# A hand-ordered attention kernel: the transposes of the score maxima, the last maximum and some conversions of operands and weights stand at other places of the order

## The chip, the cores and the metric

The kernel runs on one core of one Trainium2 chip. The metric is device time in microseconds of one execution; lower is better. "Before" ran three times: 929.05, 930.24 and 933.62 us, median 930.24 us.

## The reference: what is computed

Bucketed attention over 4 batches of 8 heads (768 positions, head size 64), then a feed-forward layer whose activation is a quotient of two polynomials.

```python
q_bits = (einsum('bhsd,dk->bhsk', q, proj) > 0)          # 6 bits, likewise k_bits
q_bucket = sum(q_bits * 2 ** arange(6), axis=-1)          # likewise k_bucket
mask = q_bucket[:, :, :, None] == k_bucket[:, :, None, :]
scores = where(mask, scale * q @ k.T, -1e9)
attn = exp(scores - max(scores)); attn = attn / (sum(attn) + 1e-9)
x = (attn @ v) as rows of B*S tokens by H*D
h = x @ w_in;  P = a0 + a1 h + a2 h^2 + a3 h^3;  Q = 1 + |b0||h| + |b1|h^2
out = (P / (Q + 1e-6)) @ w_out
```

`w_in` and `w_out` arrive as 64-bit floats and are taken apart on the chip into a high and a low fp32r part; so are q and k.

## The kernel before

**Work units.** The 32 heads are 16 pairs `p` (two heads each). A pair has 12 score steps `s` (two halves of the queries, six blocks of 128 keys) and 12 maximum steps (two heads, six blocks of 128 queries). Four kinds of TensorE work alternate:

- `scores(p, s)`: for each head two matmuls (high parts with the rows of mask and shift, then the cross terms) into one PSUM buffer `pss`; ScalarE then takes the exponential into `E`; GpSimd adds the exponentials into `acc`.
- `maxstep(p, j)`: two matmuls of high parts into a PSUM buffer `psm`, which VectorE reduces to column `j` of `m`. The maxima of pair p+1 are taken while the scores of pair p run.
- `values(p, s)`: `psv` accumulates V times `E`; the steps 0 to 5 are one group of matmuls, 6 to 11 the other.
- `shift_turn(p)`: TensorE transposes `m` (128x12) into `pst`; VectorE clamps and negates it into `mt`; `shift_rows(p)` is a DMA that puts `mt` into row 76 of q, where the scores of pair p find it.

**PSUM buffers decide what may start.** `psm` (and `psb` of the bits) come from the pool `ps_a`, which has two buffers: the matmul of one maximum can be issued when the reduction of the maximum two before it has ended. `pss`, `pst` and `psu` share the tag "s" of the pool `ps_b`, which has three buffers: a `pss` can be issued when the exponential (or, for a `pst`, the clamping) three allocations before it has ended.

**The order is written out.** All steps are put into a dictionary `plan` under a position `12 * p + s` (function `at`, lines 476 to 477; `spread` for generators), with `s` from the tables `MID`, `FIRST`, `LAST`; at the end (lines 589 to 591) the positions are run in rising order. Each engine executes its own instructions in that order, and so does SyncE, which issues nearly all DMAs. An entry such as `shift_turn=8.61` therefore means: in program order between the scores 8 and 9 of the pair before.

**Names that the change touches.** `maxima` and `maxima_steps` (positions of the twelve maxima relative to the pair two before); `low` (its second number: the subtraction that makes the low part of k, `lo<-qkf,k` on VectorE); `shift_turn` and `shift_rows`; and `weights`, two lists of positions for the generator `weights(i)` at lines 432 to 470. Even `i` is a piece of `w_in`: DMA, two ScalarE conversions with a VectorE mask (`wr<-wr`), a VectorE shift-and-or (`ws<-ws,wr`), an integer add (`CUSTOM_DVE`, `ISA` in the order), the ScalarE cast into `wi_hi`, the VectorE subtraction into `wi_lo`. Odd `i` is a piece of `w_out`; its subtraction is `wr<-ws,wr`, after which `wo_d<-wr` stores both parts. There is one piece of each in every pair.

Of the kernel before, what the change touches and what calls it, by code (L numbers as in the profile page):

```python
# [39 lines left out]

MID = dict(
    group=6, values=[0.66, 0.05], values_out=3.5, maxima=7.17,
    maxima_steps=[0, 1.15, 1.73, 2.64, 3.32, 5.08, 5.86, 6.98, 8.0, 8.84, 10.26, 11.37], sums=14.65, sums_store=17.37,
    high=[-0.41, 1.19], low=[1.06, 3.35], bits=2.81, penalties=4.05, high_move=1.9, maskrows=5.61, second_low=-2.2,
    second_high=2.69, load_v=10.99, shift_turn=8.61, shift_rows=8.82, load=9.0, recips=[20.0, 22.0, 23.0],
    weights=[[1.44, 4.0, 4.1, 5.09, 5.49, 7.11, 9.5, 9.75, 17.5], [8.05, 10, 10.65, 11.5, 12.38, 14.29, 16.34, 19.32, 21.22]],
    weights_last=[0.5, 0.8, 1.0, 1.2],
)

# [2 lines left out]
    high_move=4.53, maskrows=8.2, second_low=4.25, second_high=4.35, load_v=4.78, group=2,  # L52
    values=[2.35, 2.65, 2.32, 2.35, 0.35, 0.61], values_out=3.02, high1=[-0.27, -5.58], low1=[11.24, 4.95],
    high_move1=20.05, load2=21.89, load3=3.8, penalties1=-6.57, maskrows1=3.69,
    weights=[[-5.7, 6.64, 6.7, 11.42, 12.19, 18.75, 21.75, 38.77, 44.13], [8.03, 9.04, 9.24, 11.12, 14.81, 15.27, 15.99, 17.91, 46.81]],
    warm=6, warms=[3, 3, 3, 1, 1, 1], maxima00=[-4.26, -2.29, -4.17, 1.67, -1.15, 2.77], shift00=[2.15, 4.99],
    shift0=[3.67, 3.44], ahead=3, scores=[[3.68, 3.82, 7.26], [6.03, 8.25, 12.4]], pen01=[4.77, 14.55], comp01=3.35,
    second_high0=[-2.86, 2.12, -3.42, 3.45], load_v0=20.9, bits1=5.23, comp1=[15.82, 11.68],
    maxima0=[3.11, -1.97, -0.5, 2.14, 2.86, 3.25], turn1=[8.46, 13.26], rows1=[9.59, 14.35],
)  # L60

LAST = dict(
# [2 lines left out]
    sums=16.96, wide=8, share=11, third=0, sums14=14.69, weights14=1.44, sumst14=22.46,  # L65
# [38 lines left out]
def bucket_attention_then_rational_ffn(ctx, tc, qT, kT, v, proj, w_in, w_out, coef, consts, out):  # L104
# [56 lines left out]
    def operands_to_terms():  # L161
# [3 lines left out]

    tail.tile([P, 32], F32, tag="below", name="below")
    last = attention(tc, nc, raw, ps_b, tail, tokens, early, operands_to_terms, ffn, load, QF, KF, v, w_in, w_out, wo_d, ident, cst,
                     ones, prj, wi_hi, wi_lo, x_d, s_d, r_d, coefficients)
    ffn.rest(ctx, last)
# [3 lines left out]
def attention(ctx, tc, nc, raw, ps_b, tail, tokens, early, operands_to_terms, ffn, load, QF, KF, v, w_in, w_out, wo_d, ident, cst, ones, prj,  # L173
# [243 lines left out]
    def recips(bb):  # L417
        n = 2 * NHP * S // P
        s = tail.tile([P, n], F32, tag="rs", name=f"rs{bb}")
        nc.sync.dma_start(s, s_d[bb].rearrange("h (x c) -> (h x) c", c=n))  # L420
        yield
        z = tail.tile([P, n], F32, tag="rz", name=f"rz{bb}")
        nc.vector.tensor_scalar(out=z, in0=s, scalar1=0.0, scalar2=S * TINY, op0=ALU.is_equal, op1=ALU.mult)
        nc.vector.tensor_tensor(out=z, in0=s, in1=z, op=ALU.add)
        nc.vector.tensor_scalar(out=s, in0=s, scalar1=0.0, scalar2=1e-9, op0=ALU.is_gt, op1=ALU.mult)
        nc.vector.tensor_tensor(out=z, in0=z, in1=s, op=ALU.add)
        nc.vector.reciprocal(out=s, in_=z)
        yield
        nc.sync.dma_start(r_d[bb].rearrange("h (x c) -> (h x) c", c=n), s)
        yield  # L430
# [45 lines left out]
    def at(p, s, f, *args):  # L476
        plan.setdefault(12 * p + s, []).append((f, args))

    def spread(p, steps, gen):
        for s in steps:  # L480
            at(p, s, lambda g: next(g, None), gen)

    for p in range(NPAIR):
        mid = 0 < p < NPAIR - 1
        n = MID["group"] if mid else (FIRST if p == 0 else LAST)["group"]
        for s in range(12):
            if p > 0 or s >= FIRST["ahead"]:
                at(p, s, scores, p, s)

            if p > 1:  # L490
                at(p - 2, MID["maxima"] + MID["maxima_steps"][s] if p > 2 else FIRST["maxima2"] + FIRST["rate2"] * s, maxstep, p, s)
            if s % n == n - 1:
                for i in range(s - n + 1, s + 1):
                    at(p, s + (MID["values"][s // n] if mid else (FIRST if p == 0 else LAST)["values"][s // n]), values, p, i)
            if s % NT == NT - 1:
                at(p, s + (LAST["vout14"] if (p, s) == (NPAIR - 2, 11) else MID["values_out"] if mid else (FIRST if p == 0 else LAST)["values_out"]), values_out, p, s // NT)
        for hf in range(2):
            at(p, 6 * hf + 9, values_store, p, hf)
        if p < NPAIR - 1:
            at(p, MID["sums"] if p < NPAIR - 2 else LAST["sums14"], sums, p)  # L500
            at(p, MID["sums_store"] if p < NPAIR - 2 else LAST["sumst14"], sums_store, p)
        if p > 1:
            for t in range(2):
                at(p - 2, (MID if p > 2 else FIRST)["high"][t], high, p, t)
                at(p - 2, (MID if p > 2 else FIRST)["low"][t], low, p, t, nc.vector if p > 2 else nc.gpsimd)
            if p % 2 == 0:
                at(p - 2, (MID if p > 2 else FIRST)["bits"], bits, p)
                at(p - 2, (MID if p > 2 else FIRST)["penalties"], penalties, p)
            at(p - 2, (MID if p > 2 else FIRST)["high_move"], high_move, p)
            at(p - 2, (MID if p > 2 else FIRST)["maskrows"], maskrows, p)  # L510
        if p > 0:
            at(p - 1, (MID if p > 1 else FIRST)["second_low"], second_low, p)
            at(p - 1, (MID if p > 1 else FIRST)["second_high"], second_high, p)
            at(p - 1, (MID if p > 1 else FIRST)["load_v"], load_v, p)
        if p > 1:
            at(p - 1, MID["shift_turn"], shift_turn, p)
            at(p - 1, MID["shift_rows"], shift_rows, p)
        if p > 3:
            at(p - 4, MID["load"], load, p)
        if p % NHP == NHP - 1 and p + 1 < NPAIR:  # L520
            spread(p, MID["recips"], recips(p // NHP))
# [308 lines left out]
```

## Time and profile before

| | us |
|---|---|
| median of three runs | 930.24 |
| lowest, highest | 929.05, 933.62 |
| the profiled execution | 929.79 |
| span of the profiled execution | 928.0 |

| stage of the span (us) | TensorE busy | VectorE busy | ScalarE busy | GpSimd busy |
|---|---|---|---|---|
| 0 to 40, start | 37.29 | 27.18 | 24.72 | 23.75 |
| 240 to 280, middle of the attention | 40.00 | 35.65 | 27.32 | 30.78 |
| 360 to 400, its last two pairs | 39.39 | 34.63 | 30.89 | 27.77 |
| 440 to 480, feed-forward layer | 40.00 | 39.40 | 28.99 | 9.68 |

A pair takes 24.4 us where the bits of two pairs are made in it and 23.1 us where they are not (in the middle of the attention the first maximum of a next pair starts at 206.85, 231.70 and 254.78 us). In the timeline a row is: start, length, engine, line, operation, output tile, input tile, shapes, how many instructions were joined; in brackets the idle time of that engine ahead of it and what ended it. Matmuls overlap, so the time that one costs is the distance from its start to the next start. The granted TensorE clock was full (1.00) all through.

### The profile page before, as it was taken

Reading aid. Unit: us, or ns where it says so; the run is one execution under the profiler, and the core shown is the slowest. Engines: PE = TensorE matmul, PEld = TensorE weight load, DVE = VectorE, ACT = ScalarE, POOL = GpSimd, SP = SyncE. Lnnn points to the kernel's source line nnn. Section 1 sums busy time; section 2 is a strip of 40 time slices with the busy share of each in tenths; the row PEclk is TensorE's granted clock in tenths of the full one; section 3 lists DMA queues with packets and bytes.
Section 4 is the critical chain, followed back from the end, with each engine's and each line's share of the span. In section 5 each row is a group of like instructions: output and inputs, shape, how many; then the busy total and the mean of one; then the engine's idle time right before and its main releaser. Section 6 shows DMA issues by size and latency. Waiting matters only on the chain.

```text
span 928.0 us, 13694 instructions
## 1 busy us (share of the span) xinstructions
PE 920.8 (99%) x4678; PEld 699.9 (75%) x4678; DVE 842.0 (91%) x1029; ACT 647.6 (70%) x1229; POOL 435.8 (47%) x361
## 2 busy tenths in 40 slices
PE   8999999999999999999999999999999999999998
PEld 4666766666767676668888888888888888888886
DVE  6799889888988898888998999899999999998996
ACT  6567767676767766887767766776676677667664
POOL 5587878787788877622222232223222322232221
PEclk9999999999999999999999999999999999999999
DMA  6767878878877777545402100400040003001001
GB/s 197 214 181 219 229 230 230 223 214 212 242 212 225 229 195 233 163 155 197 163 1 81 56 1 1 136 2 0 1 137 1 1 34 102 1 1 46 1 1 46
DMA packets 51098, 111.57 MB, mean 120 GB/s; under 512 B 9330, under 2 KB 19942, under 8 KB 51028
## 3 DMA queue, kind: packets, MB, share of 16 engines
q1 hardware_dynamic: 50596, 110.34, 40.5%
q8 instruction: 37, 0.61, 0.3%
q10 hardware_dynamic: 432, 0.36, 0.1%
q14 instruction: 33, 0.27, 0.1%
HBM read 56.82 MB, written 21.17 MB: 84 GB/s over the span
## 4 chain that ended last, share of the span: by engine, by line
PE 93%; DVE 4%; DMA 1%; SPq 0%; ACT 0%; issue 0%; DVEq 0%; ACTq 0%
PE psh L93 28%; PE pso L93 28%; PE pss L93 14%; PE psv L93 12%; PE psm L93 7%; PE psu L93 2%; DVE m L93 2%; DMA wr<-w_in 1%; PE psb L93 1%; DVE ws L93 1%; DVE wr L93 0%; SPq L93 0%; PE psw L93 0%; PE pst L93 0%; ACT E L93 0%
## 5 line engine op out<-in xcount | busy, mean ns | idle before, releaser
L93 POOL TENSOR_TENSOR gl<-c,gh 128x512 fp32r<-128x512 f32 x95 | 133.2, 1402 | 387.0 <-ACT gh L93 371.0
L93 ACT ACTIVATE E<-pss 128x384 f32<-128x384 f32 x384 | 167.5, 493 | 105.8 <-PE pss L93 91.9
L93 PE MATMUL pso<-wo,gh 128*128 128x512 f32 x768 | 236.2, 390 | 0.0
L93 DVE TENSOR_REDUCE m<-psm 128x1 f32<-128x768 f32 x192 | 179.5, 948 | 31.4 <-PE psm L93 28.2
L93 POOL TENSOR_TENSOR acc<-E,E 128x384 f32<-128x384 f32 x124 | 155.6, 1273 | 85.9 <-ACT E L93 85.7
L93 PE MATMUL pss<-q,k 128*128 128x384 f32 (+2 forms) x768 | 171.3, 347 | 0.3 <-ACT E L93 0.3
L93 PEld LDWEIGHTS pso<-wo,gh 128*128 128x128 f32 x768 | 144.3, 188 | 29.9
L93 PEld LDWEIGHTS pss<-q,k 128*128 128x128 f32 (+2 forms) x768 | 134.6, 190 | 29.1 <-issue 17.0
L93 PE MATMUL psh<-xh,wi_hi 128*128 128x512 f32 x384 | 149.8, 390 | 0.0
L93 PE MATMUL psh<-xl,wi_hi 128*128 128x512 f32 x384 | 149.7, 390 | 0.0
L93 PE MATMUL psh<-xh,wi_lo 128*128 128x512 f32 x384 | 149.6, 390 | 0.0
L93 PE MATMUL pso<-wo,gl 128*128 128x512 f32 x384 | 149.1, 390 | 0.0
L93 ACT ACTIVATE h<-psh 128x512 f32<-128x512 f32 x96 | 57.4, 598 | 130.5 <-PE psh L93 130.3
L93 POOL TENSOR_TENSOR acc<-acc,E 128x384 f32<-128x384 f32 x123 | 136.6, 1129 | 5.9 <-ACT E L93 5.7
L93 DVE SCALAR_TENSOR_TENSOR c<-c,ab,r 128x512 f32<-128x512 f32 x96 | 135.6, 1413 | 0.0
L93 PE MATMUL psv<-E,v 128*64 128x385 f32 x768 | 131.9, 492 | 0.0
L93 PE MATMUL psm<-k,q 76*128 76x384 f32 (+1 forms) x384 | 102.4, 349 | 1.6 <-DVE m L93 1.0
L93 PEld LDWEIGHTS psv<-E,v 128*64 128x64 f32 x768 | 52.2, 137 | 65.3 <-issue 63.7
L93 DVE SCALAR_TENSOR_TENSOR w<-h,absb,w 128x512 f32<-128x512 f32 x96 | 74.0, 771 | 16.2 <-ACT w L93 15.9
L93 PEld LDWEIGHTS psh<-xh,wi_hi 128*128 128x128 f32 x384 | 72.1, 188 | 16.1 <-issue 1.2
L93 PEld LDWEIGHTS psh<-xh,wi_lo 128*128 128x128 f32 x384 | 72.2, 188 | 14.9
L93 PEld LDWEIGHTS psh<-xl,wi_hi 128*128 128x128 f32 x384 | 72.1, 188 | 14.9
(78 smaller groups left out, 1221.3 us busy)
## 6 DMA issues: line engine op xcount, KB each, us to landing
q<-q SPq DMA_DIRECT2D x45, 192.0 KB
k<-k SPq DMA_DIRECT2D x45, 192.0 KB
wr<-w_in SPq DMA_DIRECT2D x16, 512.0 KB
wr<-w_out SPq DMA_DIRECT2D x16, 512.0 KB
wo_d<-wr SPq DMA_DIRECT2D x16, 512.0 KB
wo<-wo_d SPq DMA_DIRECT2D x16, 512.0 KB
qkf<-qT SPq DMA_DIRECT2D x16, 384.0 KB
qkf<-kT SPq DMA_DIRECT2D x16, 384.0 KB
```

The costliest lines, as they stand in the source:

```text
L93: return self.tc.keep_in_program_order(issue(*args, **kwargs))
```

## The change

Only positions change; no instruction is added or removed.

```diff
 MID = dict(
-    maxima_steps=[0, 1.15, 1.73, 2.64, 3.32, 5.08, 5.86, 6.98, 8.0, 8.84, 10.26, 11.37], sums=14.65, sums_store=17.37,
-    high=[-0.41, 1.19], low=[1.06, 3.35], bits=2.81, ...
-    second_high=2.69, load_v=10.99, shift_turn=8.61, shift_rows=8.82, load=9.0, recips=[20.0, 22.0, 23.0],
-    weights=[[1.44, 4.0, 4.1, 5.09, 5.49, 7.11, 9.5, 9.75, 17.5], [8.05, 10, 10.65, 11.5, 12.38, 14.29, 16.34, 19.32, 21.22]],
+    maxima_steps=[0, 1.15, 1.73, 2.64, 3.32, 5.08, 5.86, 6.98, 8.0, 8.84, 10.26, 10.45], sums=14.65, sums_store=17.37,
+    high=[-0.41, 1.19], low=[1.06, 5.64], bits=2.81, ...
+    second_high=2.69, load_v=10.99, shift_turn=5.67, shift_rows=7.2, load=9.0, recips=[20.0, 22.0, 23.0],
+    weights=[[1.44, 5.63, 5.65, 5.7, 6.3, 8.3, 10.2], [8.05, 10, 10.65, 11.5, 12.38, 14.29, 17.645, 19.32, 21.22]],
 FIRST = dict(
-    ... rows1=[9.59, 14.35],
+    ... rows1=[9.59, 14.35], turn2=8.61, rows2=8.82,
...
-            at(p - 1, MID["shift_turn"], shift_turn, p)
-            at(p - 1, MID["shift_rows"], shift_rows, p)
+            at(p - 1, MID["shift_turn"] if p > 2 else FIRST["turn2"], shift_turn, p)
+            at(p - 1, MID["shift_rows"] if p > 2 else FIRST["rows2"], shift_rows, p)
```

The twelfth maximum moves from 7.17 + 11.37 - 12 = 6.54 to 7.17 + 10.45 - 12 = 5.62 of the pair before; the first group of values stands at 5 + 0.66 = 5.66, the transpose now at 5.67. Pairs 3 to 15 are transposed at the new place (13 transposes); pairs 0 to 2 stay.

On TensorE, around the first group of values in pair 3 (its scores are `pss_6_0` for step 6 and head 0, with `q_3` and `k_3`; `psm` are the maxima of pair 4, and of pair 5 from `psm_0` on; `psv_0` are the values; "x2" is two matmuls), there stood before, from the last matmuls of the group on:

```order
L93 MATMUL psv_0_1316<-E_153,v_1161 64x385 x2
L93 MATMUL pss_6_0_1329<-q_3_614,k_3_651 128x384
L93 MATMUL pss_6_0_1329<-q_3_852,k_3_853 128x384
L93 MATMUL pss_6_1_1333<-q_3_614,k_3_651 128x384
L93 MATMUL pss_6_1_1333<-q_3_852,k_3_853 128x384
L93 MATMUL psm_11_1337<-k_4_938,q_4_906 128x384 x2
L93 MATMUL pss_7_0_1341<-q_3_614,k_3_651 128x384
L93 MATMUL pss_7_0_1341<-q_3_852,k_3_853 128x384
L93 MATMUL pss_7_1_1345<-q_3_614,k_3_651 128x384
L93 MATMUL pss_7_1_1345<-q_3_852,k_3_853 128x384
L93 MATMUL psm_0_1354<-k_5_1219,q_5_1187 128x384 x2
```

and now, first ahead of the values and then from the last matmuls of the group on:

```order
L93 MATMUL psm_9_1284<-k_4_938,q_4_906 128x384 x2
L93 MATMUL pss_5_0_1288<-q_3_614,k_3_651 128x384
L93 MATMUL pss_5_0_1288<-q_3_851,k_3_852 128x384
L93 MATMUL pss_5_1_1292<-q_3_614,k_3_651 128x384
L93 MATMUL pss_5_1_1292<-q_3_851,k_3_852 128x384
L93 MATMUL psm_10_1300<-k_4_938,q_4_906 128x384 x2
L93 MATMUL psm_11_1308<-k_4_938,q_4_906 128x384 x2
L93 MATMUL psv_0_1318<-E_148,v_1161 64x385 x2
```

```order
L93 MATMUL psv_0_1318<-E_153,v_1161 64x385 x2
L93 MATMUL pst_None<-cst,m_1087 12x128
L93 MATMUL pss_6_0_1336<-q_3_614,k_3_651 128x384
L93 MATMUL pss_6_0_1336<-q_3_851,k_3_852 128x384
L93 MATMUL pss_6_1_1340<-q_3_614,k_3_651 128x384
L93 MATMUL pss_6_1_1340<-q_3_851,k_3_852 128x384
L93 MATMUL pss_7_0_1345<-q_3_614,k_3_651 128x384
L93 MATMUL pss_7_0_1345<-q_3_851,k_3_852 128x384
L93 MATMUL pss_7_1_1349<-q_3_614,k_3_651 128x384
L93 MATMUL pss_7_1_1349<-q_3_851,k_3_852 128x384
L93 MATMUL psm_0_1357<-k_5_1219,q_5_1187 128x384 x2
```

Where in pair 3 the second and third maximum of pair 5 stand there was before (and now the row `pst` is gone from there):

```order
L93 MATMUL pss_8_1_1363<-q_3_614,k_3_651 128x384
L93 MATMUL pss_8_1_1363<-q_3_852,k_3_853 128x384
L93 MATMUL psm_1_1372<-k_5_1219,q_5_1187 128x384 x2
L93 MATMUL pst_None<-cst,m_1084 12x128
L93 MATMUL psm_2_1385<-k_5_1219,q_5_1187 128x384 x2
```

`psm_11` moved from between the scores of steps 6 and 7 to directly behind `psm_10`, ahead of the values, so that the four scores 6_0, 6_1, 7_0 and 7_1 now follow each other without a maximum; the transpose `pst` stands behind the values. Its old neighbours `psm_1` and `psm_2` now follow each other directly.

On VectorE, from the ninth maximum of pair 4 on, there stood before (`lo_5` is the low part of k of pair 5, `wr_1100` and `wr_1221` pieces of `w_out` and `w_in`):

```order
L93 TENSOR_REDUCE m_1084<-psm_8_1269 128x1
L93 TENSOR_TENSOR lo_5_1273<-qkf_847,k_5_1219 128x768
L93 TENSOR_REDUCE m_1084<-psm_9_1287 128x1
L93 TENSOR_SCALAR wr_1221<-wr_1221 128x512
L93 TENSOR_TENSOR wr_1100<-ws_1101,wr_1100 128x512
L93 SCALAR_TENSOR_TENSOR ws_1222<-ws_1222,wr_1221 128x512
L93 TENSOR_REDUCE m_1084<-psm_10_1307 128x1
L93 ISA ws_1222<-wr_1221,ws_1222 128x1024
L93 TENSOR_REDUCE m_1084<-psm_11_1337 128x1
L93 TENSOR_REDUCE m_1353<-psm_0_1354 128x1
L93 TENSOR_REDUCE m_1353<-psm_1_1372 128x1
L93 TENSOR_SCALAR mt_None<-pst_None 12x128
```

and there stands now:

```order
L93 TENSOR_REDUCE m_1087<-psm_8_1269 128x1
L93 TENSOR_REDUCE m_1087<-psm_9_1284 128x1
L93 TENSOR_REDUCE m_1087<-psm_10_1300 128x1
L93 TENSOR_REDUCE m_1087<-psm_11_1308 128x1
L93 TENSOR_TENSOR lo_5_1313<-qkf_847,k_5_1219 128x768
L93 TENSOR_TENSOR wr_1104<-ws_1105,wr_1104 128x512
L93 TENSOR_SCALAR wr_1221<-wr_1221 128x512
L93 TENSOR_SCALAR mt_None<-pst_None 12x128
L93 SCALAR_TENSOR_TENSOR ws_1222<-ws_1222,wr_1221 128x512
L93 ISA ws_1222<-wr_1221,ws_1222 128x1024
L93 TENSOR_REDUCE m_1356<-psm_0_1357 128x1
```

The four reductions stand together ahead of the low part and the weights, and the clamping `mt` stands ahead of the shift-and-or.

On ScalarE, behind the exponentials of step 7 of pair 3, the cast `wi_hi` stood ahead of the exponentials of step 8; now it stands behind them, directly ahead of the two instructions that take out the values (`col`, `xo`):

```order
L93 ACTIVATE E_149<-pss_8_0_1363 128x384
L93 ACTIVATE E_149<-pss_8_1_1367 128x384
L93 CAST wi_hi<-ws_1222 128x512
L93 COPY col_0_1381<-psv_0_1318 128x1
L93 ACTIVATE xo_0_1382<-psv_0_1318,col_0_1381 128x384
L93 ACTIVATE E_150<-pss_9_0_1389 128x384
```

The first two ScalarE conversions of the `w_in` piece moved likewise, from ahead of the exponentials of step 5 to behind them. On SyncE the DMA of the row of maxima (`q<-mt`) now stands ahead of the store `wo_d<-wr` and of the next load of `w_out`; before, it stood behind both.

More of the change, by code (lines that the diff above doesn't have):

```diff
@@ L42 @@
     group=6, values=[0.66, 0.05], values_out=3.5, maxima=7.17,
-    maxima_steps=[0, 1.15, 1.73, 2.64, 3.32, 5.08, 5.86, 6.98, 8.0, 8.84, 10.26, 11.37], sums=14.65, sums_store=17.37,
-    high=[-0.41, 1.19], low=[1.06, 3.35], bits=2.81, penalties=4.05, high_move=1.9, maskrows=5.61, second_low=-2.2,
-    second_high=2.69, load_v=10.99, shift_turn=8.61, shift_rows=8.82, load=9.0, recips=[20.0, 22.0, 23.0],
-    weights=[[1.44, 4.0, 4.1, 5.09, 5.49, 7.11, 9.5, 9.75, 17.5], [8.05, 10, 10.65, 11.5, 12.38, 14.29, 16.34, 19.32, 21.22]],
+    maxima_steps=[0, 1.15, 1.73, 2.64, 3.32, 5.08, 5.86, 6.98, 8.0, 8.84, 10.26, 10.45], sums=14.65, sums_store=17.37,
+    high=[-0.41, 1.19], low=[1.06, 5.64], bits=2.81, penalties=4.05, high_move=1.9, maskrows=5.61, second_low=-2.2,
+    second_high=2.69, load_v=10.99, shift_turn=5.67, shift_rows=7.2, load=9.0, recips=[20.0, 22.0, 23.0],
+    weights=[[1.44, 5.63, 5.65, 5.7, 6.3, 8.3, 10.2], [8.05, 10, 10.65, 11.5, 12.38, 14.29, 17.645, 19.32, 21.22]],
     weights_last=[0.5, 0.8, 1.0, 1.2],
@@ L58 @@
     second_high0=[-2.86, 2.12, -3.42, 3.45], load_v0=20.9, bits1=5.23, comp1=[15.82, 11.68],
-    maxima0=[3.11, -1.97, -0.5, 2.14, 2.86, 3.25], turn1=[8.46, 13.26], rows1=[9.59, 14.35],
+    maxima0=[3.11, -1.97, -0.5, 2.14, 2.86, 3.25], turn1=[8.46, 13.26], rows1=[9.59, 14.35], turn2=8.61, rows2=8.82,
 )
```

## The prediction, made before the changed kernel ran

> **What bounds the kernel now.** I read the page's busy times first, then the timelines of TensorE, VectorE and ScalarE over two pairs in the middle of the attention.
>
> ```profile
> PE 920.8 (99%) x4678; PEld 699.9 (75%) x4678; DVE 842.0 (91%) x1029; ACT 647.6 (70%) x1229; POOL 435.8 (47%) x361
> ```
>
> TensorE works 99% of the span. A wait that the change puts in front of one of its instructions lengthens the kernel by its whole size, and a wait that it takes away shortens it; nothing else on the other engines counts unless TensorE waits for it. So the question is which TensorE instruction of the new order finds its buffer still taken. The TensorE rows of one pair, from its tenth maximum to the fourth one of the next pair (psm_9, psm_10, values, scores 6, psm_11, scores 7, psm_0, scores 8, psm_1, transpose, psm_2, scores 9, psm_3):
>
> ```profile
> 247.35 0.52 PE L93 MATMUL psm<-k,q 76*128 76x384 f32 x2
> ...
> 248.42 0.52 PE L93 MATMUL psm<-k,q 76*128 76x384 f32 x2
> 248.87 4.10 PE L93 MATMUL psv<-E,v 128*64 128x385 f32 x24
> 252.90 0.97 PE L93 MATMUL pss<-q,k 77*128 77x384 f32 x4
> 253.71 0.52 PE L93 MATMUL psm<-k,q 76*128 76x384 f32 x2
> 254.07 0.87 PE L93 MATMUL pss<-q,k 77*128 77x384 f32 x4
> 254.78 0.52 PE L93 MATMUL psm<-k,q 76*128 76x384 f32 x2
> 255.13 0.87 PE L93 MATMUL pss<-q,k 77*128 77x384 f32 x4
> 255.84 0.52 PE L93 MATMUL psm<-k,q 76*128 76x384 f32 x2
> 256.20 0.27 PE L93 MATMUL pst_None<-cst,m 128*12 128x128 f32 x1
> 256.34 0.62 PE L93 MATMUL psm<-k,q 76*128 76x384 f32 x2
> 256.80 0.87 PE L93 MATMUL pss<-q,k 77*128 77x384 f32 x4
> 257.51 0.51 PE L93 MATMUL psm<-k,q 76*128 76x384 f32 x2
> ```
>
> From start to start a maximum costs 0.36 us, four score matmuls 0.71, the group of values 4.03, the first scores behind it 0.81. One place is already at its limit, the psm_2 behind the transpose:
>
> ```profile
> 255.33 0.96 DVE L93 TENSOR_REDUCE m<-psm 128x1 f32<-128x768 f32 x1
> ...
> 256.34 0.19 PEld L93 LDWEIGHTS psm<-k,q 76*128 76x128 f32 x1 [0.23 <-DVE m L93]
> ```
>
> The reduction of psm_0 starts 0.55 after psm_0 (254.78 to 255.33), takes 0.96, and ends at 256.29; the weight load of psm_2, which takes over its buffer, starts at 256.34. So with VectorE idle and waiting, **a maximum may start 0.55 + 0.96 + 0.05 = 1.56 us after the one two before it**. A maximum that had to wait starts together with its weight load, and the next instruction follows 0.46 later (256.34 to 256.80) instead of 0.36.
>
> **Term 1, psm_11 directly behind psm_10.** From psm_9 to psm_10 are 1.07 us (247.35 to 248.42), so psm_11 would start at 1.43 and what follows it at 1.79. Its buffer is that of psm_9: it may start at 1.56, and what follows it at 2.02. That is 0.23 lost, if the reduction of psm_9 starts at once. VectorE's rows say that it will:
>
> ```profile
> 246.85 0.96 DVE L93 TENSOR_REDUCE m<-psm 128x1 f32<-128x768 f32 x1 [0.66 <-PE psm L93]
> 247.72 1.06 DVE L93 TENSOR_TENSOR lo<-qkf,k 128x768 fp32r<-128x768 f32 x1
> ...
> 249.58 0.42 DVE L93 TENSOR_SCALAR wr<-wr 128x512 int32<-128x512 int32 x1
> 249.91 1.49 DVE L93 TENSOR_TENSOR wr<-ws,wr 128x512 fp32r<-128x512 f32 x1
> 251.33 1.48 DVE L93 SCALAR_TENSOR_TENSOR ws<-ws,wr 128x512 int32<-128x512 int32 x1
> ...
> 253.60 0.68 DVE L93 CUSTOM_DVE_ANT_0 ws<-wr,ws 128x1024 uint16<-128x1024 uint16 x1
> ...
> 257.27 0.27 DVE L93 TENSOR_SCALAR mt_None<-pst_None 12x128 fp32r<-12x128 f32 x1
> ```
>
> VectorE sat idle 0.66 before it reduced psm_8, and the low part that stood behind that reduction moves away. 13 pairs have the new neighbours: 13 x 0.23 = **+3.0**. In its old place psm_11 waited for nothing, so there is nothing to gain there.
>
> **Term 2, scores 7 without a maximum ahead of them.** The three buffers of tag "s" go round: score 7_1 (second head) takes over the buffer of 6_0. ScalarE's rows for the same pair:
>
> ```profile
> 253.62 0.87 ACT L93 ACTIVATE E<-pss 128x384 f32<-128x384 f32 x2 [3.60 <-POOL acc L93]
> 254.68 0.87 ACT L93 ACTIVATE E<-pss 128x384 f32<-128x384 f32 x2 [0.20 <-PE pss L93]
> 255.44 0.62 ACT L93 CAST wi_hi<-ws 128x512 fp32r<-128x512 f32 x1
> 255.95 0.89 ACT L93 ACTIVATE E<-pss 128x384 f32<-128x384 f32 x2
> 256.70 0.18 ACT L93 COPY col<-psv 128x1 f32<-128x1 f32 x1
> ...
> 257.42 0.87 ACT L93 ACTIVATE E<-pss 128x384 f32<-128x384 f32 x2
> ...
> 254.00 0.49 ACT L93 ACTIVATE E<-pss 128x384 f32<-128x384 f32 x1
> ...
> 393.00 0.86 ACT L93 ACTIVATE E<-pss 128x384 f32<-128x384 f32 x2
> ...
> 393.92 0.66 PEld L93 LDWEIGHTS pss<-q,k 77*128 77x128 f32 x4 [0.29 <-ACT E L93]
> ```
>
> The exponential of 6_0 starts 0.72 after score 6 (252.90 to 253.62) and takes 0.49; a load that waits for an exponential follows its end by 0.06 (393.86 to 393.92). So 7_1 may start 1.27 after score 6. In the new order it would start at 0.81 + 0.35 = 1.16, and psm_0 behind it at 0.81 + 0.71 = 1.52. With the wait psm_0 starts at 1.27 + 0.46 = 1.73: 0.21 lost. Before, psm_11 gave 0.36 of cover. 13 x 0.20 = **+2.6**.
>
> **Term 3, the cast behind the exponentials of step 8.** Before, the cast ran from 255.44 to 255.95 in a gap ahead of them. Now it stands between them and `col`, `xo`, exponential 9_0. Counted from psm_0: score 8 at 0.35, its exponential 0.61 later (as 254.07 to 254.68), two exponentials 0.75, cast 0.51, `col` and `xo` 0.72: exponential 9_0 starts at 2.94, ends at 3.43. Before it started at 257.42, which is 2.64. Score 10_1 takes over that buffer and may start at 3.49, psm_4 behind it at 3.95. Unhindered it goes: psm_2 at 1.56, scores 9 at 2.02, psm_3 at 2.73, scores 10 at 3.09, 10_1 at 3.44, psm_4 at 3.80. 0.15 lost, in the 12 pairs that still have a next pair's maxima in this stretch: **+1.8**.
>
> **Term 4, the transpose.** Its departure gains nothing at the old place: psm_2 there starts when the reduction of psm_0 allows it, at 1.56, transpose or not. Behind the values no row shows it. With the two rows between its old neighbours (0.14 to the next start, then 0.46), values and scores already pay such a switch (0.81 instead of 0.71), so it would add 0.06 at most; the other transpose in the trace, below, lets the next score start 0.03 later, and by that it would gain 0.08. Bounds -1.0 and +0.8 for 13; I take 0, since both rows are equally near.
>
> Behind it, `mt` must end before score 7_0 (its buffer) and the reduction of psm_0 must start on time. From psm_10 VectorE has: reductions of psm_10 and psm_11 until about 2.4, low part 1.06, `wr` 1.42 and the mask 0.42: done at 5.0 to 5.3. The transpose ends at 0.36 + 0.23 + 0.46 + 3.9 + 0.27 = 5.2. So `mt` is hardly late, and ends near 5.6, while 7_0 is loaded at about 5.8. Then the shift-and-or and the add stand ahead of the reduction of psm_0:
>
> ```profile
> 240.98 0.69 DVE L93 SCALAR_TENSOR_TENSOR ws<-ws,wr 128x512 int32<-128x512 int32 x1
> ...
> 255.25 1.98 POOL L93 TENSOR_TENSOR acc<-E,E 128x384 f32<-128x384 f32 x2 [1.72 <-ACT E L93]
> ...
> 201.72 1.27 DVE L93 TENSOR_SCALAR wr<-wr 128x512 int32<-128x512 int32 x1
> ```
>
> The shift-and-or took 1.48 while GpSimd worked and 0.69 at 240.98. In its new place GpSimd is idle (the 1.72 ahead of 255.25), so 5.6 + 0.69 + 0.68 is about 7.0, and the reduction of psm_0 is not possible before 6.9 + 0.55 = 7.4. It is on time, and psm_2 stays as it is. The Trainium skill, "SBUF — State Buffer", section "SBUF: two separate sides", says that VectorE with two SBUF inputs and GpSimd take a shared port pair as an exclusive lock for a whole instruction. The 1.48 against 0.69 agrees.
>
> **The other moves have cover.** The two conversions on ScalarE now run during the values, where ScalarE idled 3.60 (the bracket at 253.62). `wi_lo` runs one reduction later, ahead of that of psm_4, whose buffer psm_6 takes over only behind the second group of values (4.03). The low part of k ends some 2 us later and is first read by the DMA `second_low`, at position 9.8 of the same pair. On SyncE the row of maxima goes out first, then the store, then the load of `w_out`.
>
> ```profile
> 254.30 0.34 SPq L93 DMA_DIRECT2D wr<-w_out  x1
> 257.57 0.78 SPq L93 DMA_DIRECT2D q<-mt_None  x1
> ```
>
> The load must wait for the integer add (near 7.0 instead of 5.9 after psm_10), so it leaves about 1.1 later. Its reader on ScalarE stands behind the exponentials of step 10, which are 0.4 later themselves; a late load would delay the exponentials of step 11, which TensorE needs only at the end of a 4 us group of values. I cost it at nothing.
>
> **What goes.** Two waits of the profiled run have their causes moved away:
>
> ```profile
> 208.51 0.28 PE L93 MATMUL pst_None<-cst,m 128*12 128x128 f32 x1
> 208.91 0.61 PE L93 MATMUL psm<-k,q 76*128 76x384 f32 x2
> ...
> 374.20 0.28 PE L93 MATMUL pst<-cst,m 128*12 128x128 f32 x1 [0.32 <-DVE m L93]
> ```
>
> At 208 the mask of the weights held VectorE up and psm_2 came 0.40 behind the transpose instead of 0.14: -0.26. The last transpose waited 0.32 for its reduction. Together **-0.6**.
>
> **Sum.** 3.0 + 2.6 + 1.8 + 0 - 0.6 = +6.8 us. The profiled execution took 929.8 us (span 928.0 and 1.8 around it), 0.4 below the median of the three runs. 929.8 + 6.8 = **936.6 us**.
>
> **Rivals.**
> - *The transpose's switch is what counts (faster).* Between the maxima the transpose costs 0.14 and makes the next maximum 0.46 instead of 0.36: 0.24. If it is free behind the values and the new neighbours wait for nothing, 13 x 0.24 + 0.6 = 3.7 go: 926.1 us. It decides if psm_0's reduction ends before 1.25, when the load would be due; it ends at 1.51. Chance 4%.
> - *The waits are smaller than I put them.* If only the start waits and the next instruction follows at the usual 0.36, each wait loses 0.10 less: 13 x 0.13 + 13 x 0.10 + 12 x 0.05 - 0.6 = 3.0, so 932.8 us. Against it: the load and the matmul of psm_2 start together at 256.34, and 0.46 follows. Chance 16%. The Trainium skill, "TensorE: Matmul & The Clock Gate", section "Architectural detail: the array is 16× 32×32, not 1× 128×128", has TensorE pull weight loads ahead of matmuls in flight; by that rule the load would be done before the buffer is free, which is this rival. The row at 256.34, a load held by VectorE, speaks against it.
> - *VectorE comes late.* The mask took 0.42 at 249.58, but 1.27 at 201.72. Behind `wr`, 0.85 more would make `mt` end near 6.5 and hold score 7_0 until then; 0.2 of that is already in term 2, some 0.35 is new: 13 x 0.35 = 4.6, so 941.2 us. Chance 12%.
> - *Nothing happens*, because something off these rows limits TensorE anyway: 929.8 us. 99% busy speaks against it. Chance 4%.
>
> **How the numbers follow.** The forecast has 64%, with its own range 934.6 to 938.8. The range 932.2 to 940.8 leaves out the first and last rival, the upper half of the third and some of the second. A measurement of this kernel can tell 0.5% from no change, 925.6 and 934.9 here. Faster: half of the first rival, 2%. Same: the other half, the second and the last rival and a thin tail of the forecast, 25%. Slower: 73%.
>
> **What would show it.** In the changed trace: psm_11's load idle and ended by VectorE, 1.56 after psm_9; a load of score 7_1 and one of score 10_1 that wait for ScalarE's exponentials; psm_2 still 1.56 behind psm_0; pairs some 0.6 us longer than 23.1 and 24.4. Wrong it would be if `mt` or the reduction of psm_0 came late (more), or if the pair kept its length (the buffers were free earlier than I count).

## The result, and the profile after

| | before | changed |
|---|---|---|
| median, us | 929.87 | 1023.43 |
| ratio, 95% interval | | 1.0991 (1.0954 to 1.1027) |
| the profiled execution, us | 929.79 | 1022.27 |
| its span, us | 928.0 | 1020.4 |
| mean granted TensorE clock | 1.000 | 0.946 |

The change costs 9.9%, not the 0.7% of the forecast, and the time is far above the range. The medians here and below are over all executions, while the ratios leave out two that took over 1.5% longer than the fastest of their kernel (2355.45 us of the changed kernel, 965.64 of e7). First the busy times and the row of the granted clock from the page of the changed kernel, to be set beside the first row of the prediction (TensorE 920.8, 99%).

```profile
PE 971.6 (95%) x4678; PEld 727.0 (71%) x4678; DVE 839.2 (82%) x1029; ACT 654.8 (64%) x1229; POOL 422.5 (41%) x361
...
PEclk9979879898887889879999999999999999999999
```

The same 4678 matmuls keep TensorE busy for 51 us longer, and it now idles 48.8 us instead of 7.2. Both stand in the attention stage: between 40 and 450 us of the span TensorE idles 41.9 us (before, between 40 and 370 us, 0.2), and the clock's digits fall below 9 only in the first half, where it had been full throughout.

One pair of the changed kernel, TensorE's rows in the timeline: the transpose, scores 6, scores 7, psm_0, then psm_1, psm_2, scores 9 and psm_3:

```profile
243.96 0.28 PE L93 MATMUL pst_None<-cst,m 128*12 128x128 f32 x1
243.99 0.98 PE L93 MATMUL pss<-q,k 77*128 77x384 f32 x4
245.26 1.00 PE L93 MATMUL pss<-q,k 77*128 77x384 f32 x4 [0.29 <-ACT E L93]
246.10 0.52 PE L93 MATMUL psm<-k,q 76*128 76x384 f32 x2
...
247.36 0.52 PE L93 MATMUL psm<-k,q 76*128 76x384 f32 x2
251.78 1.01 PE L93 MATMUL psm<-k,q 76*128 76x384 f32 x2 [3.90 <-DVE m L93]
252.59 1.48 PE L93 MATMUL pss<-q,k 77*128 77x384 f32 x4
253.87 0.84 PE L93 MATMUL psm<-k,q 76*128 76x384 f32 x2
```

psm_2 waits 3.90 us for a reduction. From there on the four score matmuls take 1.28 from start to start (252.59 to 253.87) instead of 0.71. VectorE's rows in the same stretch say why the reduction was late, and SyncE's queue says on what VectorE stood (its rows are DMA issues):

```profile
237.31 3.96 DVE L93 TENSOR_REDUCE m<-psm 128x1 f32<-128x768 f32 x4 [0.65 <-PE psm L93]
245.33 0.96 DVE L93 TENSOR_TENSOR lo<-qkf,k 128x768 fp32r<-128x768 f32 x1 [4.07 <-ACT E L93]
...
247.98 0.27 DVE L93 TENSOR_SCALAR mt_None<-pst_None 12x128 fp32r<-12x128 f32 x1
...
250.78 1.81 DVE L93 TENSOR_REDUCE m<-psm 128x1 f32<-128x768 f32 x2
```

```profile
240.41 0.79 SPq L93 DMA_DIRECT2D q<-mb  x1
...
242.88 0.77 SPq L93 DMA_DIRECT2D k<-mb  x1
```

The low part of k starts 4.07 us after the reduction ahead of it. The name in its bracket, an exponential, is long done; in other pairs and in a run below the same bracket names the DMA `k<-mb`. `maskrows` issues four DMAs, one for each of the two slots of q and of k; the last writes rows 64 to 76 of the slot of k that `low` subtracts. The new position of `low`, 5.64, is behind `maskrows` at 5.61, so `low` now waits for what `maskrows` wrote, where before `maskrows` stood behind `low`. It starts 2.45 us after that DMA's issue (242.88 to 245.33). The weights, the clamping and the reduction of psm_0 queue behind it on VectorE, and psm_2 waits for that reduction. In the changed kernel (and in all runs below whose low part stands behind the mask rows) the low part of k in rows 64 to 76 of one slot is thereby taken against the mask rows and no longer against the high part. `second_low` hands these rows on to the cross terms of the scores, so the move is not a mere reordering: other numbers are computed there. Over the 13 pairs the list of waits has 49.8 us of VectorE's idle time ahead of `low`, 3.1 to 6.4 us each.

The clock, in stretches of 3.41 us from 246.58 on (columns: stretch, its length, then busy time and instructions of each engine, the granted clock, the DMA share and GB/s):

```profile
246.58:249.99 3.41, 1.30 (x7) 0.89 (x6) 3.27 (x5) 1.15 (x3) 3.41 (x3) 1.00 0.01 2
249.99:253.40 3.41, 1.62 (x5) 1.62 (x6) 3.17 (x4) 1.26 (x3) 1.59 (x2) 0.50 0.81 286
253.40:256.82 3.42, 3.42 (x13) 3.42 (x12) 2.09 (x4) 2.21 (x5) 0.80 (x1) 0.50 0.76 254
256.82:260.23 3.41, 3.41 (x12) 1.59 (x12) 2.98 (x3) 2.37 (x5) 3.32 (x4) 0.50 0.47 136
260.23:263.64 3.41, 3.41 (x21) 1.59 (x18) 0.00 (x0) 0.00 (x0) 0.33 (x1) 1.00 0.98 271
```

After a stretch in which TensorE worked 1.30 of 3.41 us its clock is halved for three stretches, two of which it is busy throughout. The trace has 13 such falls between 65 and 450 us, one in each pair, 3.4 to 13.7 us long. The Trainium skill, "TensorE: Matmul & The Clock Gate", section "What's actually happening", has the clock halved after an idle window of about 3.4 us and released after a busy one; the stretches agree in length and in the factor. But the stretch ahead of this fall was not idle (1.30 us of work), and two busy ones passed ahead of the release; after the fall at 222.68 us one was enough.

### The profile page after: what moved, and what is told of

The parts are those of the page before. It is cut to its first block, busy times and chain, and to the rows that moved or that the text cites. A ratio compares the mean times of both kernels' runs of the same rounds, so it can differ in the third digit from the quotient of the medians.

```text
span 1020.4 us, 13673 instructions
## 1 busy us (share of the span) xinstructions
PE 971.6 (95%) x4678; PEld 727.0 (71%) x4678; DVE 839.2 (82%) x1029; ACT 654.8 (64%) x1229; POOL 422.5 (41%) x361
## 4 chain that ended last, share of the span: by engine, by line
PE 84%; DVE 7%; DMA 3%; issue 2%; SPq 2%; ACT 1%; POOL 1%; DVEq 0%; ACTq 0%; POOLq 0%
PE psh L93 26%; PE pso L93 26%; PE pss L93 12%; PE psv L93 10%; PE psm L93 6%; DVE ws L93 3%; DVE m L93 2%; PE psu L93 2%; DVE wr L93 2%; DMA k<-mb 2%; SPq L93 2%; PE psb L93 1%; ACT E L93 1%; DMA q<-lo 1%; PE psw L93 0%
## 5 line engine op out<-in xcount | busy, mean ns | idle before, releaser
L93 ACT ACTIVATE E<-pss 128x384 f32<-128x384 f32 x384 | 169.6, 492 | 172.3 <-PE pss L93 167.3
L93 POOL TENSOR_TENSOR acc<-E,E 128x384 f32<-128x384 f32 x124 | 150.8, 1234 | 189.0 <-ACT E L93 188.9
L93 PE MATMUL pss<-q,k 128*128 128x384 f32 (+2 forms) x768 | 194.3, 382 | 3.5 <-ACT E L93 3.5
L93 PEld LDWEIGHTS pss<-q,k 128*128 128x128 f32 (+2 forms) x768 | 150.4, 214 | 33.0 <-ACT E L93 11.0
L93 PE MATMUL psm<-k,q 76*128 76x384 f32 (+1 forms) x384 | 113.6, 383 | 40.1 <-DVE m L93 39.0
L93 PE MATMUL psv<-E,v 128*64 128x385 f32 x768 | 146.1, 531 | 0.3 <-ACT E L93 0.3
L93 POOL TENSOR_TENSOR acc<-acc,E 128x384 f32<-128x384 f32 x123 | 127.7, 1057 | 8.8 <-ACT E L93 7.7
L93 PEld LDWEIGHTS psm<-k,q 76*128 76x128 f32 (+1 forms) x384 | 74.9, 211 | 56.2 <-DVE m L93 51.6
L93 PEld LDWEIGHTS psv<-E,v 128*64 128x64 f32 x768 | 56.4, 149 | 78.1 <-issue 74.2
```

The lines of the kernel that those rows point to most:

```text
L93: return self.tc.keep_in_program_order(issue(*args, **kwargs))
```

## The experiments

Theory A: the low part behind the mask rows makes VectorE wait for a DMA, TensorE for VectorE, and the idle TensorE loses its clock. Rival B: the short new waits or the transposes among the values do it. In each diff only what differs is shown; times are medians, with the ratio to the kernel before, which took 930.8 to 931.1 us alongside them, and its 95% interval.

| run | us | ratio |
|---|---|---|
| e1_low_first | 936.0 | 1.005 (1.0038 to 1.0061) |
| e2_low_alone | 958.8 | 1.0275 (1.0241 to 1.0309) |
| e3_maxima_alone | 960.4 | 1.0305 (1.0286 to 1.0325) |
| e4_weights_alone | 930.8 | 0.9997 (0.9987 to 1.0006) |
| e5_filled_wait | 1011.4 | 1.0856 (1.0829 to 1.0882) |
| e6_k_mask_second | 969.1 | 1.0403 (1.038 to 1.0426) |
| e7_k_mask_first | 957.2 | 1.0251 (1.0208 to 1.0293) |
| e8_waits_spread | 933.8 | 1.0033 (1.0018 to 1.0047) |
| e9_low_old_place | 944.6 | 1.0154 (1.014 to 1.0167) |
| e10_waits_spread_more | 937.4 | 1.0081 (1.006 to 1.0102) |

**e1: the changed kernel, only that `low` comes ahead of `maskrows`.**

```diff
-    ... low=[1.06, 5.64], ... maskrows=5.61,
+    ... low=[1.06, 5.64], ... maskrows=5.65,
```

> The changed kernel with one number changed: the mask rows stand at 5.65 instead of 5.61, so they come behind the low part of k (5.64) again, as before the change; all other moves stay. Theory A (the low part of k reads the rows that the mask-row DMAs write, VectorE stands about 4 us for their landing in 13 pairs, psm_2 comes 4 us late and the granted clock then falls to half): without that order the 92 us go but for the small waits of the prediction, some 3.0 for psm_11, 13 x 0.46 = 6.0 for score 7, up to 1.8 for the cast, so 930 + 6 to 11 = 936 to 941 us, full clock all through. Rival B (the new short waits of TensorE, or the transpose and its clamping among the values, trip the clock by themselves): stays at 1000 us or more, with the clock still falling in each pair.

936.0 us, full clock: theory A. The other 87 us hang on the order of two steps 0.03 apart. Its busy times, then TensorE's rows of a pair (psm_10 and psm_11 joined, values, transpose, scores 6 and 7 joined, psm_0, scores 9, scores 10, psm_4), then VectorE's reductions of psm_8 to psm_11 and of psm_0 to psm_3:

```profile
PE 926.1 (99%) x4678; PEld 697.3 (75%) x4678; DVE 825.4 (88%) x1029; ACT 649.5 (70%) x1229; POOL 421.2 (45%) x361
```

```profile
251.56 1.11 PE L93 MATMUL psm<-k,q 76*128 76x384 f32 x4
252.60 4.10 PE L93 MATMUL psv<-E,v 128*64 128x385 f32 x24
256.63 0.28 PE L93 MATMUL pst_None<-cst,m 128*12 128x128 f32 x1
256.67 1.86 PE L93 MATMUL pss<-q,k 77*128 77x384 f32 x8
258.36 0.52 PE L93 MATMUL psm<-k,q 76*128 76x384 f32 x2
...
260.39 0.88 PE L93 MATMUL pss<-q,k 77*128 77x384 f32 x4
...
261.46 0.92 PE L93 MATMUL pss<-q,k 77*128 77x384 f32 x4
262.22 0.52 PE L93 MATMUL psm<-k,q 76*128 76x384 f32 x2
```

```profile
249.98 3.95 DVE L93 TENSOR_REDUCE m<-psm 128x1 f32<-128x768 f32 x4 [0.66 <-PE psm L93]
...
258.92 3.75 DVE L93 TENSOR_REDUCE m<-psm 128x1 f32<-128x768 f32 x4 [0.26 <-PE psm L93]
```

VectorE now waits for psm_0 (the 0.26), not psm_2 for VectorE's backlog. This run also splits the 87 us. Against it the changed kernel has 971.6 - 926.1 = 45.5 us more busy time for the same matmuls, which is the half clock (TensorE is busy for 94.5 us within the 13 falls, and half of that is 47), and (1020.4 - 971.6) - (933.7 - 926.1) = 41.2 us more idle time, which is the waiting: together 86.7, the difference of the spans (e1's is 933.7).

**e2: the kernel before with only `low` moved behind `maskrows`.**

```diff
-    ... low=[1.06, 3.35],
+    ... low=[1.06, 5.64],
```

> The kernel before with the low part of k at 5.64 instead of 3.35, alone: it stands behind the mask rows (5.61). The low part of k is then taken, in rows 64 to 76 of head 1, against the mask rows instead of the high part. Theory A: VectorE waits for the DMA's landing in 13 pairs and TensorE for VectorE, so 990 to 1025 us with a granted clock that falls in each pair. Rival B (the cause lies in the maxima and the transpose): 930 us, full clock. Rival C (both are needed, since before the change the maxima psm_9 to psm_11 still had VectorE work between them): in between, waits of 1 to 3 us and a full clock, 940 to 970 us.

958.8 us is the size of rival C, not the 990 to 1025 of theory A. The wait is there, but shorter, for the weights still stand ahead of `low` on VectorE and fill a part of it. One of its rows, and the sum over the trace in the list of waits (us, times, longest):

```profile
245.25 0.96 DVE L93 TENSOR_TENSOR lo<-qkf,k 128x768 fp32r<-128x768 f32 x1 [1.70 <-DMA k<-mb]
...
DVE lo L93 <- DMA k<-mb: 18.5, 10, 3.4
```

In this profiled execution, the fastest of four with 950.2 us, the clock fell once, early in the attention, and was full afterwards (mean 0.995). The other three took 958 to 960 us at a mean clock of 0.986 to 0.988, so rival C's full clock did not hold either.

**e3: the kernel before with only the last maximum and the transposes moved.**

```diff
-    maxima_steps=[..., 10.26, 11.37], ... shift_turn=8.61, shift_rows=8.82,
+    maxima_steps=[..., 10.26, 10.45], ... shift_turn=5.67, shift_rows=7.2,
```

> The kernel before with the last maximum at 10.45 and the transpose and rows of maxima at their new places (pairs 3 to 15), and nothing else. Theory A: psm_11 waits 0.23 and score 7 some 0.46 in 13 pairs, 3.0 + 6.0, less up to 0.6: 936 to 939 us, full clock. By the prediction's own size of the second term (0.20): 934 to 936 us. Rival B: 1000 us or more. If the transpose's switch between maxima counted: 926 us.

960.4 us: neither theory had it. The forecast's waits of 0.23 hold only if VectorE has nothing else to do; here the low part and the weights still stand between the reductions:

```profile
238.94 0.62 PE L93 MATMUL psm<-k,q 76*128 76x384 f32 x2 [0.66 <-DVE m L93]
...
244.43 0.28 PE L93 MATMUL pst_None<-cst,m 128*12 128x128 f32 x1 [0.84 <-DVE m L93]
```

psm_11 waits 0.66, and the transpose, which needs the last reduction, 0.84. The clock fell twice late in the attention, for 3.4 us each (mean 0.996). So the move of the weights is no ornament: it is what brings the 960 down to e1's 936, together with the low part's (e9 below parts the two).

**e4: the kernel before with only the weights' positions changed.**

```diff
-    weights=[[1.44, 4.0, 4.1, 5.09, 5.49, 7.11, 9.5, 9.75, 17.5], [..., 14.29, 16.34, ...]],
+    weights=[[1.44, 5.63, 5.65, 5.7, 6.3, 8.3, 10.2], [..., 14.29, 17.645, ...]],
```

> The kernel before with only the positions of the weights' steps changed (the cast of a piece of w_in behind the exponentials of step 8, conversions behind those of step 5, the weights' VectorE work moved). Prediction's third term: score 10_1 waits 0.15 in 12 pairs, 931 to 933 us, full clock. Rival: VectorE's mask, which takes up to 1.27 us, stands ahead of a reduction that TensorE waits for: 935 us or more. Or nothing: 930 us.

Nothing: 930.8. By itself the cast behind the exponentials of step 8 costs no time that can be measured.

**e5: the changed kernel with psm_1's two matmuls issued eleven times in pairs 3 to 15.**

```diff
-        for hf in range(2):
+        for hf in range(2) if j != 1 or p < 3 else 11 * (0, 1):
```

> The changed kernel, with the two matmuls of psm_1 issued eleven times in a row instead of once in pairs 3 to 15 (the same numbers into the same buffer): 10 x 0.36 = 3.6 us of TensorE work stand where it waited 3.8 us for the late reduction of psm_0, behind the same late low part of k. Theory A1 (the 92 us are some 4 us of waiting in 13 pairs, and the rest is the half clock that the wait brings on): the clock stays full, only the wait itself remains, so 936 + 13 x 3.6 to 4.1 = 983 to 989 us. Rival A2 (the clock is a side effect; VectorE, behind by 4 us, is what makes the rest of the pair slow): 1010 us or more.

As a number, 1011 fits A2's bound and not A1's. The rows say more. The same wait on VectorE, now with the DMA named, TensorE's row of the filled place, and two pairs as stretches (from one transpose to the next), first of this run and then of the changed kernel:

```profile
253.85 0.96 DVE L93 TENSOR_TENSOR lo<-qkf,k 128x768 fp32r<-128x768 f32 x1 [3.82 <-DMA k<-mb]
...
256.11 3.99 PE L93 MATMUL psm<-k,q 76*128 76x384 f32 x22
...
252.70:281.90 29.20, 28.64 (x175) 19.92 (x174) 21.11 (x24) 17.48 (x38) 18.48 (x16) 1.00 0.65 184
281.90:309.50 27.60, 27.30 (x159) 19.43 (x158) 21.39 (x28) 16.64 (x37) 17.17 (x16) 1.00 0.66 193
```

```profile
244.00:277.20 33.20, 29.01 (x157) 19.33 (x155) 21.69 (x24) 17.70 (x38) 18.22 (x16) 0.85 0.56 161
277.20:306.10 28.90, 26.97 (x139) 17.75 (x137) 20.80 (x28) 16.86 (x37) 17.45 (x16) 0.88 0.63 184
```

With TensorE kept busy and VectorE as late as before, the clock is full and the pair with the bits takes 29.2 us instead of 33.2. So the slow matmuls come from TensorE's idling, not from VectorE. What A1 had wrong is that the filler fits every pair. In the changed kernel the pair at 277 idles 28.90 - 26.97 = 1.93 us and that at 244 4.19, so 3.6 us of filler are too much for the one, while in three places (at 65, 140 and 202 us) the clock still fell, for 6.8 to 20.5 us. Against e1 the profiled run has 988.0 - 926.1 = 61.9 us more busy time, of which 13 x 3.6 = 47 are the filler and the other 15 these falls, and 12.7 us more idle time; together they are the 74.6 us between the spans.

**e6 and e7: the mask rows of the slot that `low` reads issued second, then first.**

```diff
 def maskrows(p, queues=(None, None)):
-    for h in range(2):
+    for h in (1, 0):
...
-        move(nc, Q1[p][64:76, h, :], ...)
-        move(nc, K1[p][64:77, h, :], ...)
+        move(nc, K1[p][64:77, h, :], ...)
+        move(nc, Q1[p][64:76, h, :], ...)
```

The first edit alone is e6, both are e7.

> The changed kernel with the mask rows of head 1 moved ahead of those of head 0 (order q1, k1, q0, k0 instead of q0, k0, q1, k1). The low part of k reads only slot 1, so it waits for the second DMA instead of the fourth, issued 1.63 us earlier. Theory A: VectorE's wait falls from 4.07 to about 2.4 us, psm_2 is some 2.2 us late. By the waits alone, with the clock falling as before: 1023 - 13 x 1.63 = 1002 us; if a wait of 2 us no longer brings the clock down: 936 + 13 x 2.2 = 965 us. Rival (the wait is not for the landing of the rows in slot 1, but for all mask rows or for the exponential that the trace names): 1020 us, unchanged.

> As the run before it, with k ahead of q as well (order k1, q1, k0, q0): the low part of k waits for the first of the four DMAs, 2.4 us earlier than in the changed kernel. Theory A: VectorE's wait falls from 4.07 to about 1.6 us, psm_2 is 1.4 us late, the clock stays full: 936 + 13 x 1.4 = 954 us. If VectorE's idle time ahead of psm_0's reduction (0.26 in the run with the low part first) and its shorter instructions take some of it up: 945 us. Rival: 1020 us, unchanged.

969 and 957 us, within 5 us of the 965 and 954 of theory A. VectorE's wait for the DMA shrinks as the DMA moves forward from the fourth place to the second and the first, a row of e6 and one of e7:

```profile
230.30 0.96 DVE L93 TENSOR_TENSOR lo<-qkf,k 128x768 fp32r<-128x768 f32 x1 [2.42 <-DMA k<-mb]
```

```profile
242.22 0.96 DVE L93 TENSOR_TENSOR lo<-qkf,k 128x768 fp32r<-128x768 f32 x1 [1.24 <-DMA k<-mb]
```

In these rows `low` starts 2.60 and 2.78 us after the issue of that DMA (227.70 and 239.44), against 2.45 in the changed kernel. Over the 13 pairs, waits of 49.8, 33.8 and 21.4 us ahead of `low` give 1023, 969 and 957, and no wait gives 936. It is the landing of the rows in that one slot. The time falls faster than the wait, since the clock now falls in only four places of e6 (mean 0.981) and two of e7 (0.993). Theory A's 965 and 954 were worked out with full clock, so that they agree to 5 us is partly luck; the four executions of e7, from 950 to 966 us, go with their clocks, from 0.995 down to 0.984.

**e8 and e10: can the version with the low part first beat the kernel before?**

```diff
 # e8, from e1
-    maxima=7.17, maxima_steps=[0, 1.15, ..., 8.0, 8.84, 10.26, 10.45],
+    maxima=7.004, maxima_steps=[0, 1.316, ..., 8.166, 9.0, 10.0, 10.616],
...
-                at(p, s, scores, p, s)
+                if mid and s in (4, 5, 7):
+                    at(p, s, scores, p, s, (0,))
+                    at(p, s + 0.008, scores, p, s, (1,))
+                else:
+                    at(p, s, scores, p, s)
 # e10, from e8: 1.316 -> 1.0, s in (4, 5, 7, 8), and in weights 5.7 -> 5.665
```

> A version that the runs so far point to: the low part of k ahead of the mask rows (maskrows 5.65), the transposes behind the values, and three maxima moved between the two heads' scores of a step in the middle pairs, psm_9 inside step 4, psm_10 inside step 5, psm_0 inside step 7. Then psm_10 and psm_11 start 0.71 apart and psm_11 1.78 after psm_9 (no wait: 1.56 is needed), score 7_1 has the 0.36 of psm_0 ahead of it, and psm_2 comes 1.78 behind psm_0. If the three waits are what the 936 us still hold over 931: 936.0 - 13 x (0.23 + 0.17 + 0.23) = 927.8 us, 0.3% under the kernel before. If the new order brings waits of its own (VectorE not ready for psm_0, which comes 0.5 us earlier, or the mask rows not landed): 936 us or more.

> The version with the spread maxima, with two more edits: psm_1 inside step 8 between the heads, and the shift-and-or of w_in ahead of the clamping on VectorE, where VectorE idled 0.38, so that psm_0's reduction, which came 0.2 late behind the integer add, is on time. If the waits of psm_2 and psm_3 (0.18 and 0.10 each for the slower start) are what is left: 933.8 - 13 x 0.56 = 926.5 us, 0.5% under the kernel before. If only one of the two goes: 930 us. If the clamping comes later and holds a score's buffer, or psm_1's reduction waits behind psm_0's: 934 us or more.

No. e8 wins 2.2 of the 8.2 us, e10 loses them again. The waits moved on: first weight loads of e8 (psm_2, psm_3, a score of step 10), then of e10.

```profile
233.51 0.30 PEld L93 LDWEIGHTS psm<-k,q 76*128 76x128 f32 x2 [0.18 <-DVE m L93]
234.70 0.30 PEld L93 LDWEIGHTS psm<-k,q 76*128 76x128 f32 x2 [0.18 <-DVE m L93]
235.57 0.30 PEld L93 LDWEIGHTS pss<-q,k 77*128 77x128 f32 x2 [0.22 <-ACT E L93]
```

```profile
209.93 0.30 PEld L93 LDWEIGHTS pss<-q,k 77*128 77x128 f32 x2 [0.30 <-DVE mt_None L93]
214.46 0.30 PEld L93 LDWEIGHTS pss<-q,k 77*128 77x128 f32 x2 [0.70 <-ACT E L93]
```

In e10 the maxima no longer wait; instead the clamping, moved behind the shift-and-or, holds score 7_0, and a score of step 10 waits 0.70 for an exponential behind the cast. No version tried is faster than the kernel before.

**e9: the changed kernel with `low` at its old place.**

```diff
-    ... low=[1.06, 5.64],
+    ... low=[1.06, 3.35],
```

> The changed kernel with the low part of k back at its old place (3.35), all other moves kept: VectorE then has the low part between the reductions of psm_8 and psm_9, but no weights' work there. Theory A (only the place behind the mask rows is costly): no wait for the DMA, full clock; the reduction of psm_9 ends some 0.75 us later than with the low part at 5.64, so psm_11 waits 0.75 more in 13 pairs: 936 + 9.8 = 946 us. If VectorE's idle 0.66 us ahead of psm_8's reduction takes it up: 936 us. Rival (the low part's new place was needed to keep VectorE in time for the transposes): 960 us, as with the maxima alone.

944.6, full clock, as theory A has it (946). The low part between the reductions of psm_8 and psm_9 makes psm_11's weight load wait 1.11. The run e3, which has the weights at their old places besides, is 15.8 us slower still.

```profile
258.65 0.30 PEld L93 LDWEIGHTS psm<-k,q 76*128 76x128 f32 x2 [1.11 <-DVE m L93]
```

## Why the prediction was wrong

**The step that failed** is under "The other moves have cover": "The low part of k ends some 2 us later and is first read by the DMA `second_low`, at position 9.8 of the same pair." It asked who reads the low part, and never what the low part itself must wait for in its new place. It was costed at nothing; e1 against the changed kernel puts it at 87 us. The numbers for it stood in the trace of before, in SyncE's queue:

```profile
249.80 0.79 SPq L93 DMA_DIRECT2D q<-mb  x1
...
252.33 0.78 SPq L93 DMA_DIRECT2D k<-mb  x1
```

In that pair the reduction of psm_8 starts at 246.85. In e1 the four reductions end 3.95 after that start, which is 250.80 here. The DMA of 252.33 would be usable 2.45 later, as after, at 254.78: a wait of 4.0, and 4.07 was measured. That 2.45 is no row of before, but the issue at 252.33 alone already bounds the wait in this pair from below at 1.5 us (252.33 - 250.80).

**The sum without that step was right.** It came to 936.6; e1, which is the change without it, took 936.0 (its profiled span is 5.7 above that of before). That the two agree to 0.6 us is partly luck: against the runs of before taken alongside it (930.98) e1 costs 5.0 us and not 6.8.

- *Term 1, psm_11 (+3.0).* In e1 values start 1.04 after psm_10 (251.56 to 252.60), which is 0.36 + 0.45 and 0.23 of waiting. Right.
- *Term 2, score 7 (+2.6).* psm_0 starts 1.69 after score 6 (256.67 to 258.36), predicted 1.73, unhindered 1.52: 13 x 0.17 = 2.2. Right. In the changed kernel itself the wait is larger: there score 7_0, and not 7_1, starts 1.27 after score 6 (243.99 to 245.26), when the exponential of 6_0 has ended, and the two steps take 2.11 (243.99 to 246.10). The prediction has 7_0 take over the buffer of the transpose; here it took that of 6_0, and why, no run shows.
- *Term 3, the cast (+1.8).* Too large: in e1 psm_4 comes 0.76 after score 10 (261.46 to 262.22; 0.71 unhindered), 12 x 0.05 = 0.6, and e4 shows none.
- *Term 4, the transpose (0, between -1.0 and +0.8).* Behind the values the next score starts 0.04 after it (256.63 to 256.67): 13 x 0.04 = +0.5. psm_2 still starts when the reduction of psm_0 allows it, and what follows it stands 2.03 behind psm_0 (258.36 to 260.39), 2.02 before.
- *What goes (-0.6).* With it the terms make 3.0 + 2.2 + 0.6 + 0.5 - 0.6 = 5.7, e1's difference in span; the -0.6 itself was not measured apart.
- *"`mt` is hardly late", "It is on time, and psm_2 stays as it is".* True in e1 (VectorE idles 0.26 ahead of psm_0's reduction), false in the changed kernel, where both queue behind the low part: the clamping starts 4.02 after the transpose (243.96 to 247.98).
- *The rivals.* None came true. The third had VectorE late, but by a mask of 1.27 us. None had an engine wait for a DMA, and none had TensorE's clock fall, since the trace of before shows it full all through.

## What to carry to other kernels

For each step that is moved, list not only who reads its result but also what it reads, and look whether it now passes a step that writes the same buffer, in place, by DMA: the wait then turns round. Price the turned wait from the queue that issues the DMAs (the last one's issue plus its landing) against the time at which the engine comes by. And where TensorE is the bound, idle time of more than about 1.2 us within 3.41 us (the least that a fall followed here, see below) is to be priced twice, once as itself and once for the clock that it may cost. Also ask whether the moved step now reads other contents, for then it computes something else.

## What was not expected of the hardware

How little idling it takes. Two stretches of 3.41 us of the changed kernel, then two of e3:

```profile
280.71:284.12 3.41, 1.78 (x10) 1.46 (x10) 3.41 (x4) 2.15 (x6) 3.41 (x4) 1.00 0.69 213
284.12:287.54 3.42, 3.42 (x12) 3.00 (x10) 2.51 (x4) 1.68 (x5) 2.09 (x3) 0.50 0.93 345
```

```profile
261.17:264.59 3.42, 2.22 (x13) 1.86 (x11) 3.42 (x4) 1.28 (x4) 3.42 (x4) 1.00 0.84 186
264.59:268.00 3.41, 2.83 (x16) 1.36 (x18) 2.55 (x5) 1.99 (x4) 1.47 (x2) 1.00 0.46 120
```

In the changed kernel a wait of 1.63 us that lay within one stretch (TensorE busy 1.78 of 3.41) was followed by half clock. In e3 a wait of 1.78 us that began in one stretch and ended in the next (busy 2.22 and 2.83) was not. The falls of one run start at multiples of 3.41 us from each other, so it seems to be the share of a fixed stretch that counts. Of the 13 stretches ahead of the changed kernel's falls the busiest, from 434.30 on, had 2.19 of 3.41, so in the attention stage the limit would lie between 2.19 and 2.22. That is not the whole rule: at the end of e4 a stretch with 1.96 of 3.40 (from 922.90 on) was followed by full clock. No run was made for that alone. The Trainium skill, "TensorE: Matmul & The Clock Gate", section "HAM oscillation — how this bites in real kernels", gives as its rule no idle gap over about 3.4 us; the 1.63 here is half of that, so for this kernel the measurement decides.
